# Windowed attention feeding a routed expert layer: where a running count is taken, an order of its own behind the last slot, and a normalization moved between engines

## Chip, core and metric

The kernel runs on one core of a Trainium2 chip. The metric is the device time of one execution, in microseconds (us), as the median of three executions. The engines are PE (TensorE, matrix products), DVE (VectorE), ACT (ScalarE), POOL (GpSimd) and SP (SyncE, which here only issues transfers). Each engine works through its own queue in order.

## The reference, cut to what matters

```
# attention: 8 batches, 8 heads, 576 positions, head size 64, window of 128 positions
scores = where(0 <= i - j < 128, q k^T / 8 - slope_h * |i - j|, -1e9)
x = softmax(scores) @ v                       # (8, 576, 512)
# expert layer: 8 experts, hidden size 1024
logits = x @ w_gate
for every token: fresh = argmax(logits)
    e = fresh if first of its batch or sigmoid(x . w_local) < 0.5 else e of the token before
    out = softmax(logits)[e] * (relu(x @ w1[e]) @ w2[e])
```

Each token goes to one expert, so the second half is a gather of token rows by expert, two matrix products, and a scatter.

## The kernel before, in words

**Attention.** Two heads make a pair and a batch has four pairs, so there are 32 pairs, numbered 0 to 31. The work of a pair is cut into atoms, each a letter and a block number: S (scores, PE), D (bias and row minimum, DVE), E (exponential and row sum, ACT), A and R (reciprocal of the sums: POOL, then DVE), N (the pieces of the block row times the reciprocal, nine in all, N3 four and N8 five), U (transposes, PE), C (their copy out of PSUM, DVE or ACT), M and H (products with v, PE), X (copy into the tile `xT`) and T (32x32 transposes of `xT` into the tile `T`, DVE). After a batch's fourth pair, T0 and T1 are each followed by a transfer of `T` to DRAM (`xd`): 1024 KB for T0, 128 KB for T1. There is one tile `T`, so a T of the next batch waits until these transfers have read it.

**Slots.** A slot emits one list of atoms, a software pipeline: an atom with k marks (`M3'''` has three) belongs to the pair k-1 before that of an unmarked one. `ORDER` holds the lists for the four pairs of a batch. Behind the last pair `LAST` holds what the pipeline still owes. Every engine gets its instructions in the order in which the atoms stand (`InOrder`, whose helper is L170 in the profile).

**Side work.** A `.` in a list takes one step of a generator, `side`: `tokens(b)` computes logits of a finished batch and `route(b)` the expert of each token, its rank among that expert's tokens (with `ohs`, the running count by expert) and the lists of rows. `;`, `:` and `,` take steps of `early()`, `gathers()` and `turns()`, which prepare the rows of the first expert before attention ends. `early()` rounds the count of an expert up to a whole tile at three points, after batches 3, 4 and 5: one PE product adds `ohs` up over partitions (`pn`), and three DVE operations follow. All these small PSUM results use one bank, `ptk` with `bufs=1`, so PE can write the next only when the last one has been read.

**Experts.** `Fixed.run` goes over eight pieces f of the hidden size: twelve products h (`three` four times), a relu on ACT (`hh`) and DVE (`hl`, L1101), and then nine products y of the piece before. Weights are loaded as `wraw` (512 KB), split by ACT (cast) and DVE (L246, the low part), two halves for each. `hl` lies where `T` lay, so the second `hl` waits until the last transfer out of `T` has landed. `Feed.tick` takes steps of `routing()` (tokens and route of the last batch, then the lists of all experts), gathers rows on POOL (L185) and turns them on DVE (L191, L195).

Of the kernel before, what the change touches and what calls it, by code (L numbers as in the profile page):

```python
# [8 lines left out]
F32 = mybir.dt.float32  # L9
# [4 lines left out]
ALU = mybir.AluOpType  # L14
AX = mybir.AxisListType
PS = bass.MemoryType.PSUM
P = 128

NB = 8
S = 576  # L20
DM = 512
NE = 8
NT = 5
KS = 4
NS = 3
# [11 lines left out]
EARLY = [[(2, 4), (3, 5)], [(3, 6)]]  # L37
# [13 lines left out]
def windows(nb):  # L51
    last = nb % 4
    if last in (1, 2):
# [14 lines left out]
]  # L68
DEPTH = 4
FIRST = "S0 S2 D2 D0 D1 D3 S8 D8 S4 S6 E8"  # L70
LAST = ["E2' M3''' E1' T1'''' D6' D4' C0''' . D5' D7' E0' . H2''' H0''' H3''' N8'' H1''' N3'' M1''' E3' E6' E5' E7' M0''' . U2'' E4' A3' C2'' U3'' . C3'' U1'' A8' T0'''' X0''' X1''' U0'' M2'' C1'' R3' R8'",
# [3 lines left out]
POOL_CUT = 19  # L75
PACE = 16
GROUP = 3
# [5 lines left out]
def moe_attention(ctx, tc, qT, kT_d, vv, wg, wl, w1, w2, out):  # L83
# [6 lines left out]
    tp = ctx.enter_context(tc.tile_pool(name="tok", bufs=2))  # L90

    sh = ctx.enter_context(tc.tile_pool(name="shared", bufs=2))
    ptk = ctx.enter_context(tc.tile_pool(name="ptk", bufs=1, space=PS))
# [11 lines left out]
    onesb = cp.tile([P, P], F16, name="onesb")  # L105
# [20 lines left out]
    ohs = st.tile([P, NE], F16, name="ohs")  # L126
    g32 = st.tile([P, 32], F32, name="g32")
    tbl = st.tile([P, 4 * NS * KS], F32, name="tbl")
# [17 lines left out]
    def chain(*gens):  # L146
        for g in gens:
            yield from g

    def run(g):  # L150
        for _ in g:
            pass
# [23 lines left out]
    pe, dve, act, pool = (InOrder(e) for e in (nc.tensor, nc.vector, nc.scalar, nc.gpsimd))  # L176
# [168 lines left out]
    with ExitStack() as actx:  # L345
# [168 lines left out]
        class Scores:  # L514


            def __init__(self, b, p, q, k):
                self.p, self.q, self.k, self.pbs = p, q, k, PB[(4 * b + p) % 2]
                self.mn = sp.tile([P, 9], F32, name="mn", bufs=3)
                self.sm = sp.tile([P, 9], F32, name="sm", bufs=3)  # L520
                self.r = sp.tile([P, 9], F32, name="r", bufs=3)
                self.ps, self.sc = {}, {}
# [43 lines left out]

            def N(self, i):
                for j in range(0, 4) if i == 3 else range(4, 9):
                    pool.tensor_scalar(self.part(j), self.part(j), self.r[:, j:j + 1], 1.0, ALU.mult, ALU.mult)

        class Weigh:
# [80 lines left out]
        def route(b):  # L652
            L = logits_of.pop(b)
            l8 = L[:, :, 0:NE]
            OH, RO = oh_all[:, b], ro_all[:, b]
# [36 lines left out]
            dve.tensor_tensor(OH, ph, k8, ALU.is_equal)  # L692
            yield

            assert all((e, k) in known for e, parts in enumerate(EARLY) for k, n in parts if n <= b)
            pr = ptk.tile([P, NT, NE], F32, name="pk")
            pe.matmul(pr, utri, OH, start=True, stop=False)
            for t in range(1, NT):
# [16 lines left out]
            for a in range(4):  # L715
                n = NT if a < 2 else NT - 1
# [24 lines left out]
                if t % 2:  # L741
                    yield
            yield
            pT = ptk.tile([P, 4 * NS * KS], F32, name="pk")
            for t in range(NT):
                pe.matmul(pT, RO[:, t], cw[:, t].rearrange("p e k -> p (e k)"), start=t == 0, stop=t == NT - 1)
            yield
            enter(tbl, pT, b)
            routed.append(b)
            yield  # L750

        def enter(table, ps, b):

            base = float(S * (b - b % GROUP))
            if base:
                z = tp.tile([P, P], F32, name="tz")[:, :table.shape[1]]
                dve.tensor_scalar(z, ps, 0.0, base, ALU.is_gt, ALU.mult)
            dve.tensor_tensor(table, table, ps, ALU.add)
            if base:
                dve.tensor_tensor(table, table, z, ALU.add)  # L760
# [43 lines left out]
        def early():  # L804

            parts = [(n, e, k, k0) for e, own in enumerate(EARLY) for (k, n), (k0, _) in zip(own, [(0, 0)] + own)]
            for n, e, k, k0 in sorted(parts):
                while n - 1 not in routed:
                    yield
                pn = ptk.tile([P, NE], F32, name="pk")  # L810
                pe.matmul(pn, onesb, ohs, start=True, stop=True)
                d = tp.tile([P, 1], F32, name="ed")
                dve.tensor_scalar(d, pn[:, e:e + 1], -1.0, float(k * P), ALU.mult, ALU.add)
                dve.tensor_scalar(d, d, 0.0, None, ALU.max)
                dve.tensor_tensor(ohs[0:1, e:e + 1], ohs[0:1, e:e + 1], d[0:1], ALU.add)
                yield
                at = 4 * KS * e + 4 * k0
                yield from indices(tbl[:, at:at + 4 * (k - k0)], idx0, at, KS * e + k0, windows(4 * (k - k0)))
                known.append((e, k))
# [53 lines left out]
        for slot in range(4 * NB + DEPTH):  # L873
# [30 lines left out]
                loaded = load(b + 1)  # L904
            if p == 2 and b + 1 < NB:
                load_v(b + 1)
        run(chain(prep[";"], prep[":"], prep[","], side))
        last_xT = xT


# [279 lines left out]
    class Flex:  # L1190
        n = 1
# [85 lines left out]
    route_done, rank_done, table_done, beyond = [], [], [], []  # L1277

    def routing():
        yield from chain(tokens(NB - 1, last_xT), route(NB - 1))  # L1280
        e = len(OWN) - 1
        yield from indices(tbl[:, 4 * KS * e:4 * KS * e + 4 * KS], idxs, 0, 0, windows(4 * KS))
        route_done.append(1)
        yield
        yield from rank_tables()
        table_done.append(1)
# [132 lines left out]
```

## Time and profile before

| | us |
|---|---|
| median of 3 | 667.01 (666.23 to 667.06) |
| the profiled execution: its own time | 666.91 |
| its span, first to last instruction | 665.1 |
| PE busy | 636.6 (96%), mean granted clock 0.982 |
| DVE busy | 455.5 (68%) |
| ACT busy | 393.4 (59%) |
| POOL busy | 390.5 (59%) |

The profiled execution stands 0.10 below the median, and 1.8 us of its time lie outside the span. The shares are averages over a kernel of two halves: attention ends at about 222 us, and what follows is expert work.

### The profile page before, as it was taken

To read this page: it belongs to the slowest core of one execution; us is meant where nothing else is said; L and a number is where in the kernel's file an instruction comes from. 1 tells how busy PE (TensorE), PEld (TensorE's weight loads), DVE (VectorE), ACT (ScalarE), POOL (GpSimd) and SP (SyncE) were. 2 spreads that over 40 slices of the span, in tenths; PEclk is the share of its full clock that TensorE was granted. 3 is DMA by queue.
4 is the path that set the end of the run, shared out by engine and by line. 5 is a ranking of instruction groups with operands and counts; after the bars stand their busy time and mean duration, and the time that the engine had idled before them with its cause. 6 is when DMAs were issued, how large, how long until landed. Compare 5 with 4: busy or idle time off the path is not lost. (4 is left out here: it accounts for less than half of the span.)

```text
span 665.1 us, 18079 instructions
## 1 busy us (share of the span) xinstructions
PE 636.6 (96%) x6414; PEld 526.2 (79%) x6414; DVE 455.5 (68%) x1623; ACT 393.4 (59%) x1177; POOL 390.5 (59%) x651
## 2 busy tenths in 40 slices
PE   8899999999977899999999999999999999999994
PEld 4677777776755688888887898888988899889883
DVE  4679999999996788994654374637464667854531
ACT  7899999988976444353443353535353565653430
POOL 6866666667859741776777575765253476615021
PEclk9999999999986999999999999999999999999998
DMA  8976765665212654557424673448333488448420
GB/s 274 369 260 204 234 188 182 210 194 184 81 51 78 204 175 150 189 178 238 133 69 150 206 247 96 138 155 269 124 114 117 145 264 318 143 136 298 158 85 30
DMA packets 59757, 117.01 MB, mean 176 GB/s; under 512 B 9132, under 2 KB 28076, under 8 KB 59664
## 3 DMA queue, kind: packets, MB, share of 16 engines
q1 hardware_dynamic: 50096, 95.93, 44.1%
q0 software_dynamic: 9136, 19.30, 8.9%
q8 instruction: 52, 0.85, 0.5%
q10 hardware_dynamic: 432, 0.59, 0.3%
q14 instruction: 41, 0.34, 0.2%
HBM read 96.84 MB, written 19.29 MB: 175 GB/s over the span
## 5 line engine op out<-in xcount | busy, mean ns | idle before, releaser
L185 POOL DMA_INDIRECT kr<-xd,xidx x136 | 147.4, 1084 | 52.1 <-issue 37.3
L1048 PE MATMUL h<-qx,cut 128*128 128x384 f32 (+6 forms) x408 | 136.2, 334 | 0.0
L170 POOL TENSOR_SCALAR cut<-cut,r 128x192 f32<-128x192 f32 (+2 forms) x288 | 114.4, 417 | 35.2 <-DVE r L170 15.3
L246 DVE TENSOR_TENSOR cut<-wraw,cut 128x512 fp32r<-128x512 f32 x171 | 110.8, 686 | 34.5 <-ACT cut L244 29.4
L1050 PE MATMUL h<-qx,cut 128*128 128x384 f32 (+6 forms) x408 | 134.4, 329 | 0.0
L1049 PE MATMUL h<-qx,cut 128*128 128x384 f32 (+6 forms) x408 | 134.2, 329 | 0.0
L170 ACT ACTIVATE cut<-scs,mn 128x192 f32<-128x192 f32 (+2 forms) x288 | 123.1, 433 | 6.0 <-DVE mn L170 4.5
L1042 POOL DMA_INDIRECT out<-y,sidx x41 | 45.4, 1108 | 133.9 <-ACT y L1057 65.3
L1100 ACT ACTIVATE hh<-h 128x384 fp32r<-128x384 f32 (+3 forms) x96 | 44.4, 463 | 126.3 <-PE h L1050 125.3
L1101 DVE SCALAR_TENSOR_TENSOR hl<-h,hh 128x384 fp32r<-128x384 f32 (+3 forms) x104 | 54.2, 521 | 93.1 <-ACT hh L1100 90.0
L1048 PE MATMUL y<-cut,hh 128*128 128x512 f32 x288 | 114.1, 396 | 0.0
L1049 PE MATMUL y<-cut,hh 128*128 128x512 f32 x288 | 114.1, 396 | 0.0
L1050 PE MATMUL y<-cut,hl 128*128 128x512 f32 x288 | 113.6, 395 | 0.0
L244 ACT CAST cut<-wraw 128x512 fp32r<-128x512 f32 x148 | 84.2, 618 | 26.9 <-PE y L1050 24.7
L170 DVE CUSTOM_DVE_ANT_0 scs<-sc,bias 128x192 f32<-128x192 f32 (+2 forms) x288 | 84.1, 318 | 6.8 <-PE sc L170 5.8
L1048 PEld LDWEIGHTS h<-qx,cut 128*128 128x128 f32 x408 | 77.0, 189 | 8.7 <-issue 4.1
L1049 PEld LDWEIGHTS h<-qx,cut 128*128 128x128 f32 x408 | 77.0, 189 | 4.3
L1050 PEld LDWEIGHTS h<-qx,cut 128*128 128x128 f32 x408 | 76.9, 189 | 1.9
L1050 PEld LDWEIGHTS y<-cut,hl 128*128 128x128 f32 x288 | 54.5, 189 | 11.9
L170 PE MATMUL pt<-ident,cut 128*128 128x128 f32 x384 | 60.7, 289 | 2.9 <-POOL cut L170 2.8
L170 PE MATMUL sc<-kr,qx 64*64 64x192 f32 (+2 forms) x1280 | 62.0, 303 | 1.0 <-DVE mn L170 0.6
L1048 PEld LDWEIGHTS y<-cut,hh 128*128 128x128 f32 x288 | 54.5, 189 | 9.1 <-issue 0.4
(214 smaller groups left out, 1079.8 us busy)
## 6 DMA issues: line engine op xcount, KB each, us to landing
wraw<-w SPq DMA_DIRECT2D x92, 512.0 KB
xT<-w SPq DMA_DIRECT2D x20, 512.0 KB
kr<-kT SPq DMA_DIRECT2D x31, 288.0 KB
qx<-qT SPq DMA_DIRECT2D x30, 288.0 KB
cut<-v SPq DMA_DIRECT2D x8, 1024.0 KB
xd<-T SPq DMA_DIRECT2D x8, 1024.0 KB
kr<-xd,xidx POOLq DMA_INDIRECT x136, 3.7
cut<-v SPq DMA_DIRECT2D x8, 128.0 KB
```

The source lines that it names most:

```text
L170: ins = getattr(self.engine, name)(*args, **kw)
L185: queued(nc.gpsimd.indirect_dma_start(out=r, out_offset=None, in_=src[0:n, :], in_offset=bass.IndirectOffsetOnAxis(ap=col, axis=0), bounds ...
L244: scalar.copy(c[:, 0, f], raw[:, f])
L246: (pool if 2 * n + f == POOL_CUT else vector).tensor_tensor(c[:, 1, f], raw[:, f], c[:, 0, f], ALU.subtract)
L1042: queued(nc.gpsimd.indirect_dma_start(out=out.rearrange("t (a c) -> (t a) c", a=n), out_offset=bass.IndirectOffsetOnAxis(ap=col, axis=0), ...
L1048: nc.tensor.matmul(o, ah, bh, start=start, stop=False)
L1049: nc.tensor.matmul(o, ah, bl, start=False, stop=False)
L1050: nc.tensor.matmul(o, al, bh, start=False, stop=stop)
L1100: now.act.activation(hh, hp[:, :M], AF.Relu)
L1101: nc.vector.scalar_tensor_tensor(hl, hp[:, :M], 0.0, hh, ALU.max, ALU.subtract)
```

## The change

Three things change. First, the product that counts (`pn`) leaves `early()` and is made at the end of `route(b)`, in further columns of the tile `pT` that takes the lists; the three DVE operations follow there. Second, `DEPTH` goes from 4 to 1: the four lists of `LAST` become one, in which pairs 28 to 31 stand mixed and a `.` comes after every six atoms; what is left of `side` behind it is no longer run out at once but handed to `routing()`. Third, the nine N pieces of pair 31 are DVE operations instead of POOL ones.

```diff
-DEPTH = 4
+DEPTH = 1
...
-        ". M3''' T1'''' C0''' . H2''' H0''' H3''' N8'' T0'''' H1''' N3'' M1''' . M0''' U2'' C2'' . U3'' C3'' U1'' X0''' X1''' U0'' M2'' C1'' .",
...
+LAST = ["T0'''' M1''' N3'' E0' M3''' E1' . H1''' H2''' T1'''' H3''' C0''' E2' . E3' D4' M0''' N8'' D5' H0''' . E4' U0'' D6' X1''' X0''' C0'' . E5' E6' T0''' M0'' A3' U1'' . T1''' D7' U2'' R3' C1'' N3' . U3'' C2'' M1'' C3'' U0' M2'' . E7' C0' M3'' H0'' A8' H1'' . H2'' R8' H3'' N8' X0'' X1'' . M0' U1' T0'' U2' C1' U3' . T1'' C2' M1' C3' M2' M3' . H0' H1' H2' H3' X0' X1' . T0' T1'"]
...
+                self.last = 4 * b + p >= 4 * NB - 1
...
             def N(self, i):
                 for j in range(0, 4) if i == 3 else range(4, 9):
+                    if self.last:
+                        dve.tensor_scalar(self.part(j), self.part(j), self.r[:, j:j + 1], None, ALU.mult)
+                        continue
                     pool.tensor_scalar(self.part(j), self.part(j), self.r[:, j:j + 1], 1.0, ALU.mult, ALU.mult)
...
-            pT = ptk.tile([P, 4 * NS * KS], F32, name="pk")
+            pT = ptk.tile([P, 4 * NS * KS + NE], F32, name="pk")
             for t in range(NT):
-                pe.matmul(pT, RO[:, t], cw[:, t].rearrange("p e k -> p (e k)"), start=t == 0, stop=t == NT - 1)
-            yield
-            enter(tbl, pT, b)
+                pe.matmul(pT[:, :4 * NS * KS], RO[:, t], cw[:, t].rearrange("p e k -> p (e k)"), start=t == 0, stop=t == NT - 1)
+            full = [(e, k) for e, parts in enumerate(EARLY) for k, n in parts if n == b + 1]
+            if full:
+                pe.matmul(pT[:, 4 * NS * KS:], onesb, ohs, start=True, stop=True, skip_group_check=True)
+            yield
+            enter(tbl, pT[:, :4 * NS * KS], b)
+            for e, k in full:
+                d = tp.tile([P, 1], F32, name="ed")
+                at = 4 * NS * KS + e
+                dve.tensor_scalar(d, pT[:, at:at + 1], -1.0, float(k * P), ALU.mult, ALU.add)
+                dve.tensor_scalar(d, d, 0.0, None, ALU.max)
+                dve.tensor_tensor(ohs[0:1, e:e + 1], ohs[0:1, e:e + 1], d[0:1], ALU.add)
             routed.append(b)
             yield
...
-                pn = ptk.tile([P, NE], F32, name="pk")
-                pe.matmul(pn, onesb, ohs, start=True, stop=True)
-                d = tp.tile([P, 1], F32, name="ed")
-                dve.tensor_scalar(d, pn[:, e:e + 1], -1.0, float(k * P), ALU.mult, ALU.add)
-                dve.tensor_scalar(d, d, 0.0, None, ALU.max)
-                dve.tensor_tensor(ohs[0:1, e:e + 1], ohs[0:1, e:e + 1], d[0:1], ALU.add)
-                yield
...
-        run(chain(prep[";"], prep[":"], prep[","], side))
+        run(chain(prep[";"], prep[":"], prep[","]))
+        rest = side
...
     def routing():
-        yield from chain(tokens(NB - 1, last_xT), route(NB - 1))
+        yield from chain(rest, tokens(NB - 1, last_xT), route(NB - 1))
```

How this moves instructions is shown at three places. The first is DVE's queue at the end of slot 31, the last slot with scores, from the routing step `rcb` of batch 6 on. Before:

```order
L170 TENSOR_TENSOR rcb<-rc,rf 128x5
L170 STREAM_TRANSPOSE T<-xT 128x2x32
L170 ISA scs,mn<-sc,bias 128x192
L170 ISA mn 128x1
L170 TENSOR_TENSOR xT<-wraw,xT 128x512
L170 ISA scs,mn<-sc,bias 128x192
L170 ISA mn 128x1
L170 COPY pts<-pt 128x384
```

With the change (lines of the helpers stand three lower there, L167 for L170):

```order
L167 TENSOR_TENSOR rcb<-rc,rf 128x5
L167 STREAM_TRANSPOSE T<-xT 128x16x32
L167 TENSOR_TENSOR xT<-wraw,xT 128x512
L167 STREAM_TRANSPOSE T<-xT 128x2x32
L167 COPY pts<-pt 128x384
L167 TENSOR_TENSOR xT<-wraw,xT 128x512
L167 SCALAR_TENSOR_TENSOR hr_99<-hold,pk 1x512
L167 ISA scs,mn<-sc,bias 128x192
```

The 16-block transpose into `T` (T0 of pair 28, the first pair of batch 7), which stood eleven instructions further on, is now the first behind `rcb`; the D atoms of pair 31 (`scs,mn`) stand behind it.

The second place is DVE's queue where pair 31 is normalized (`cut` times `r`). Before, these nine rows were POOL's. With the change:

```order
L167 RECIPROCAL r<-r 128x4
L167 TENSOR_SCALAR cut<-cut,r 128x64
L192 TENSOR_TENSOR qx<-xtr,qx 128x4x128
L167 TENSOR_SCALAR cut<-cut,r 128x128
L167 TENSOR_SCALAR cut<-cut,r 128x192 x2
L167 TENSOR_TENSOR rex<-L,rm 128x40
L167 TENSOR_TENSOR oh_all<-pk,k_85 128x40
L167 COPY pts<-pt 128x384
```

N3 stands as three rows there, and N8 follows in the same way behind the next reciprocal.

The third place is the first expert, where PE turns the logits of batch 7 (`pk<-ident,part`, five products, the fifth after DVE has read the first four, `L<-pk`). PE before:

```order
L1050 MATMUL h<-qx,cut 128x384
L1048 MATMUL h<-qx,cut 128x384
L1049 MATMUL h<-qx,cut 128x384
L1050 MATMUL h<-qx,cut 128x384
L1048 MATMUL h<-qx,cut 128x384
L170 MATMUL pk<-ident,part 128x128
L1049 MATMUL h<-qx,cut 128x384
L1050 MATMUL h<-qx,cut 128x384
```

PE with the change:

```order
L1051 MATMUL y<-cut,hh 128x512
L1052 MATMUL y<-cut,hh 128x512
L1053 MATMUL y<-cut,hl 128x512
L1051 MATMUL h<-qx,cut 128x384
L167 MATMUL pk<-ident,part 128x128
L1052 MATMUL h<-qx,cut 128x384
L1053 MATMUL h<-qx,cut 128x384
```

The fifth product stood behind seven of the twelve products h of piece f=2; it now stands behind those twelve, the nine products y of f=1 and one product h of f=3. DVE before, from the first `hl`:

```order
L1101 SCALAR_TENSOR_TENSOR hl<-h,hh 128x384
L246 TENSOR_TENSOR cut<-wraw,cut 128x512 x2
L1101 SCALAR_TENSOR_TENSOR hl<-h,hh 128x384
L246 TENSOR_TENSOR cut<-wraw,cut 128x512 x4
L170 TENSOR_REDUCE L<-pk 128x36
```

DVE with the change, from the last rows of batch 7 in `T`:

```order
L167 STREAM_TRANSPOSE T<-xT 128x16x32
L167 STREAM_TRANSPOSE T<-xT 128x2x32
L167 TENSOR_SCALAR ro_all<-rep_91,rrf,val 128x128 x3
L167 TENSOR_SCALAR tz<-pk 128x48
L167 TENSOR_TENSOR tbl<-tbl,pk 128x48
L167 TENSOR_TENSOR tbl<-tbl,tz 128x48
L1104 SCALAR_TENSOR_TENSOR hl<-h,hh 128x384
L243 TENSOR_TENSOR cut<-wraw,cut 128x512 x2
L1104 SCALAR_TENSOR_TENSOR hl<-h,hh 128x384
L243 TENSOR_TENSOR cut<-wraw,cut 128x512 x6
L1104 SCALAR_TENSOR_TENSOR hl<-h,hh 128x384
L243 TENSOR_TENSOR cut<-wraw,cut 128x512 x2
```

The row `L<-pk` stands next behind these. Between the second `hl` and it there were four splits (L246) and are now six, a third `hl` and two more splits.

## Rows read from the trace of the kernel before

**Rows 1.** Busy time by engine, ten-microsecond stretches (stretch, length, busy and count each, PE's granted clock).

```profile
core 0: us, PE busy (x) PEld busy (x) DVE busy (x) ACT busy (x) POOL busy (x), PEclk, DMA share, GB/s
...
200.00:210.00 10.00, 6.45 (x86) 4.41 (x83) 6.20 (x17) 7.44 (x26) 8.97 (x15) 0.73 0.39 116
...
240.00:250.00 10.00, 10.00 (x60) 8.69 (x59) 8.23 (x28) 4.15 (x9) 1.30 (x1) 1.00 0.32 100
```

**Rows 2.** Who waited for whom on PE: total us, times, longest.

```profile
PE pk L170 <- DVE tbl L170: 3.4, 3, 2.4
PE pk L170 <- DVE L L170: 2.9, 1, 2.9
```

**Rows 3.** PE in order of time: start, us, and idle time before (in brackets).

```profile
27.12 0.27 PE L170 MATMUL xa<-pts,cut 64*64 64x64 f32 x2 [1.76 <-DVE pts L170]
...
190.68 0.17 PE L170 MATMUL pk<-ohs,onesb 128*128 128x8 f16 x1 [2.37 <-DVE tbl L170]
...
230.74 0.33 PE L170 MATMUL pk<-ident,part 128*128 128x128 f32 x1 [2.93 <-DVE L L170]
```

**Rows 4.** PE busy and its granted clock behind the first two of these.

```profile
core 0: us, PE busy (x), PEclk, DMA share, GB/s
...
28.00:30.00 2.00, 2.00 (x35) 1.00 1.03 403
...
192.00:194.00 2.00, 2.00 (x14) 0.50 0.03 10
```

**Rows 5.** DVE in order of time, end of slot 31.

```profile
195.32 0.36 DVE L170 CUSTOM_DVE_ANT_0 scs<-sc,bias 128x192 f32<-128x192 f32 x1 [0.56 <-PE sc L170]
...
195.88 0.70 DVE L170 STREAM_TRANSPOSE T<-xT 128x512 f32<-128x512 f32 x1
...
199.33 0.17 DVE L170 TENSOR_TENSOR rcb<-rc,rf 128x5 f16<-128x5 f32 x1
```

**Rows 6.** SP's issues of the 1024 KB transfers out of T, batches 6 and 7.

```profile
196.61 0.38 SPq L627 DMA_DIRECT2D xd<-T  x1
...
221.98 0.39 SPq L627 DMA_DIRECT2D xd<-T  x1
```

**Rows 7.** DVE in order of time, end of attention and start of the first expert.

```profile
218.89 1.25 DVE L170 TENSOR_SCALAR ro_all<-rep,rrf,val 128x128 f16<-128x128 f16 x5
...
220.69 0.16 DVE L170 TENSOR_SCALAR tz<-pk 128x48 f32<-128x48 f32 x1
...
221.12 0.83 DVE L170 STREAM_TRANSPOSE T<-xT 128x64 f32<-128x64 f32 x2
221.88 0.52 DVE L1101 SCALAR_TENSOR_TENSOR hl<-h,hh 128x384 fp32r<-128x384 f32 x1
...
227.50 0.56 DVE L1101 SCALAR_TENSOR_TENSOR hl<-h,hh 128x384 fp32r<-128x384 f32 x1 [2.55 <-DMA xd<-T]
227.98 2.49 DVE L246 TENSOR_TENSOR cut<-wraw,cut 128x512 fp32r<-128x512 f32 x4
230.38 0.30 DVE L170 TENSOR_REDUCE L<-pk 128x36 f32<-128x144 f32 x1
```

**Rows 8.** DVE's busy time from the end of slot 31 to the first hl.

```profile
core 0: us, DVE busy (x), PEclk, DMA share, GB/s
199.41:221.88 22.47, 16.99 (x61) 0.77 0.29 86
```

**Rows 9.** Groups of instructions: a DVE scaling of an SBUF tile, and POOL's N pieces.

```profile
L170 DVE TENSOR_SCALAR bias<-rel 64x256 f32<-64x256 f32 x2 | 0.6, 302 | 2.6 <-POOL rel L170 2.5
L170 POOL TENSOR_SCALAR cut<-cut,r 128x192 f32<-128x192 f32 x224 | 93.8, 435 | 35.2 <-DVE r L170 15.3 <-PE pt L170 10.3 <-DVE ti L170 9.3
```

**Rows 10.** PE in order of time, first and tenth product after the wait for L: nine products y.

```profile
231.79 0.57 PE L1048 MATMUL y<-cut,hh 128*128 128x512 f32 x1
...
235.43 0.34 PE L1048 MATMUL h<-qx,cut 128*128 128x384 f32 x1
235.61 0.34 PE L1049 MATMUL h<-qx,cut 128*128 128x384 f32 x1
```

**Rows 11.** The third expert: its list (DVE), scatter and last of 16 gathers (POOL), first product (PE).

```profile
257.57 0.23 DVE L170 TENSOR_SCALAR xidx<-fi,roff 128x16 int32<-128x16 f32 x1
...
263.46 1.03 POOL L1042 DMA_INDIRECT out<-y,sidx  x1 [4.38 <-ACT y L170]
...
287.61 1.95 POOL L185 DMA_INDIRECT kr<-xd,xidx  x1 [0.30 <-issue]
...
298.69 0.39 PE L1048 MATMUL h<-qx,cut 128*128 128x512 f32 x1
```

More of the change, by code (lines that the diff above doesn't have):

```diff
@@ L68 @@
 ]
-DEPTH = 4
+DEPTH = 1
 FIRST = "S0 S2 D2 D0 D1 D3 S8 D8 S4 S6 E8"
-LAST = ["E2' M3''' E1' T1'''' D6' D4' C0''' . D5' D7' E0' . H2''' H0''' H3''' N8'' H1''' N3'' M1''' E3' E6' E5' E7' M0''' . U2'' E4' A3' C2'' U3'' . C3'' U1'' A8' T0'''' X0''' X1''' U0'' M2'' C1'' R3' R8'",
[3 rows of a table removed]
+LAST = ["T0'''' M1''' N3'' E0' M3''' E1' . H1''' H2''' T1'''' H3''' C0''' E2' . E3' D4' M0''' N8'' D5' H0''' . E4' U0'' D6' X1''' X0''' C0'' . E5' E6' T0''' M0'' A3' U1'' . T1''' D7' U2'' R3' C1'' N3' . U3'' C2'' M1'' C3'' U0' M2'' . E7' C0' M3'' H0'' A8' H1'' . H2'' R8' H3'' N8' X0'' X1'' . M0' U1' T0'' U2' C1' U3' . T1'' C2' M1' C3' M2' M3' . H0' H1' H2' H3' X0' X1' . T0' T1'"]
 POOL_CUT = 19
@@ L693, in route @@
             yield
-            assert all((e, k) in known for e, parts in enumerate(EARLY) for k, n in parts if n <= b)
             pr = ptk.tile([P, NT, NE], F32, name="pk")
```

2 rows, old and new, of the table LAST are left out of this document.

## The prediction

> **What bounds the kernel now.** I read the busy time by stretches first. From 240 us on PE works without a break (10.00 of 10.00 us, granted clock 1.00, which is 2.4 GHz), and so it stays nearly to the end; between 200 and 210 us, where attention drains, PE is busy 6.45 of 10 us at a mean clock of 0.73 [rows 1]. So the end of the kernel moves by whatever PE gains or loses before about 240 us, as long as the later expert work is never starved. PE's waits show two of interest: 3.4 us in three waits on the table `tbl`, which are the three counts of `early()`, and 2.9 us in one wait for `L` [rows 2]. In order of time, the longest count wait ends at 190.68, after 2.37 us, and the wait for `L` at 230.74, after 2.93 us [rows 3]. A wait costs more than itself when the clock falls behind it: after the 2.37 us the clock is 0.50 (1.2 GHz) at 192 to 194 us, while after a wait of 1.76 us that ended at 27.12 it stayed 1.00 [rows 3, 4]. The same fall stands behind the wait for `L`: nine products y take 231.79 to 235.43, 3.64 us [rows 10], where nine at the full clock take 2.1 (an estimate from the last rows there: products of 384 columns start 0.18 us apart, so of 512 columns 0.24).
>
> **The count.** It removes no work: the product and three small DVE operations per count stay. What goes is PE standing before the bank until DVE has put the lists into `tbl`. PE does not get 3.4 us for that. DVE is what PE waits for there, and the next product into that bank, the logits of batch 6, still has to wait until DVE has read lists and count. What DVE itself can win in slot 31 is its wait for PE of 0.56 us at 195.32 [rows 5]. I take that, less about 0.3 us for list operations that now come ahead of the T transpose of 195.88: that transpose ends some 0.2 us earlier, and the transfer that SP issued at 196.61 [rows 6] goes at about 196.4. If the three waits were returned in full it would be 3.4 us; both ends stay for the range.
>
> **The head of DVE's queue.** With the change the 16-block transpose of pair 28 follows `rcb`, which ends at 199.5 [rows 5]. It overwrites `T`, so it must wait until the 1024 KB of batch 6 have left. How long that transfer takes is read from its twin: issued at 221.98, it let the second `hl` start at 227.50, so 5.5 us [rows 6, 7]. Issued at 196.4 it frees `T` at 201.9. DVE then stands still for about 2.5 us, and behind it in the queue stand both splits of the expert's weights, the copy `pts` that PE's M0 needs, the scan of the routing, and the D atoms of pair 31. Before, a small transpose stood there that did not wait.
>
> **DVE's work from there.** Between 199.41 and the first `hl` at 221.88 DVE is busy 16.99 of 22.47 us, so it idles 5.5 us [rows 8]. The same operations stand behind the transpose now, plus the nine N pieces. No row shows N on DVE. The nearest DVE row scales 256 elements from SBUF to SBUF in 302 ns; the nine pieces hold 1536 elements, which is 1.8 us by elements and 2.7 by instructions (9 x 0.302). I take 2.1. POOL's own price is the upper bound, 9 x 0.435 = 3.9 [rows 9]; the lower is half of the element count, 0.9. For waits between engines that a queue this full still has (the copy of U0 of pair 31 waits for PE) I add an estimate of 0.5. First `hl`: 201.9 + 17.0 + 2.1 + 0.5 = 221.5, against 221.88. So the tail itself comes out nearly even: what mixing the pairs saves, DVE gives back in the wait at its head and in the nine pieces.
>
> A rule of the Trainium skill speaks about the price. "VectorE: DVE Perf Modes" (Mode 2×_2P — use both read ports for one tensor) says that a scaling of one fp32 tensor in SBUF writes two results a cycle; the row above, 302 ns for 256 elements, is nearer to one. By the rule the nine pieces would be about 1 us cheaper (an estimate) and the sum lower by as much; I keep the row.
>
> **The first expert.** The last 16-block transpose into `T` now stands ahead of the small one, three of the five `ro_all` and the table update. These took 0.2, 0.75 (three fifths of 1.25) and 0.4 us [rows 7], so it ends at 221.5 - 1.4 = 220.1, is issued at 220.15 as the first of the two transfers, and lands 5.5 us later at 225.65 (before: 227.50). Then DVE runs to `L`: `hl` 0.5, six splits 3.6 (four took 2.40, from 227.98 to 230.38), the third `hl` 0.5, two splits 1.2, `L` 0.3 [rows 7]. That is 6.1 us, and `L` is there at 231.75, a microsecond later than before (230.68). But PE has done more by then: the last five products h of f=2, the nine y of f=1 and the first h of f=3. Before, PE was at that point, about to start the second h of f=3, at 235.61 [rows 10]. With the change it is there at 231.75 + 0.05 + 0.1 (the fifth product into the bank) = 231.9, if the clock holds behind the wait. Gain 3.7 us.
>
> Does it hold? PE's work from the first `hl` to that point is 18 products y and 13 h (18 x 0.235 + 13 x 0.175 = 6.5 us), with logits and transposes 0.8 more, after `hl` at 222.0: PE arrives at 229.3 and waits 2.4 us. That is nearest to the 2.37 us after which the clock fell, not to the 1.76 us after which it held [rows 3, 4]. I take the fall, 3.64 - 2.1 = 1.5 us as before. Gain 3.7 - 1.5 = 2.2 us.
>
> **What hides the rest.** The rest of the routing of batch 6 is no longer run out at once, so routing of batch 7 and the lists come about one piece f later in PE's order, some 4.3 us. The cover: the third expert's list was there at 257.57, the gathers were held back by the scatter at 263.46, and 16 of them were issued by 289.6, while PE needs the rows at 298.69 [rows 11]. With the change the scatters come first and the gathers follow in one run, so 262 is early enough. Beyond some 8 us of delay the third expert would start late.
>
> **Sum.** The profiled execution took 666.91 us, 0.10 below the median. 666.9 - 2.2 = **664.7 us**.
>
> **Rivals.**
> 1. *The clock holds* behind the wait for `L`, because it comes out nearer 1.8 than 2.4 us (a microsecond off either way is within the sums above): 666.9 - 3.7 = 663.2.
> 2. *The count comes back.* PE, not DVE, sets slots 22, 26 and 30, and the 3.4 us of [rows 2] return in full, no low clock at 192 us included: 664.7 - 3.4 = 661.3. Against it: DVE was the one waited for.
> 3. *No change.* DVE takes POOL's price for N (1.8 us more), which moves the first `hl`, the last transfer and `L` alike: 664.7 + 1.8 = 666.5, within 0.2% of before. For it: DVE is the full queue of this stretch and takes work from an engine with a later deadline.
> 4. *Slower.* DVE's pieces and POOL's gathers shut each other out. In the changed order POOL starts its gathers (about 1.0 us each, 1.3 apart) just when DVE does N8. If each of the five pieces waits for one gather, DVE is 5 us later, `L` too: 664.7 + 5 = 669.7. It decides against the change once the nine pieces together cost over about 4.3 us (2.1 and the gain of 2.2). Against it: the five scalings `ro_all` at 218.89 took 0.25 us each, with no sign of being held [rows 7]. "SBUF — State Buffer" of the Trainium skill (SBUF: two separate sides) has this rule: the two engines share a pair of ports as an exclusive lock, for a DVE operation in a two-port mode among others. Whether N runs in one no row shows.
>
> **Chances.** Forecast 0.37, rival 1 0.20, rival 2 0.14, rival 3 0.17, rival 4 (and late lists) 0.12. What a measurement of this kernel can tell from no change is about 0.2%, 1.3 us. The forecast's own range is 663.4 to 666.2: a landing of 5.0 to 5.9 us counts twice (0.5 each way), N 0.9 to 2.7 us. Faster by over 0.2% (below 665.6): rivals 1 and 2 and most of the forecast, 0.69. Within: rival 3 and the rest of the forecast, 0.20. Slower: 0.11. The range of 8 in 10 leaves out rival 4 and the far end of rival 2: 661.4 to 667.2.
>
> **What would show it.** Right: no wait on `tbl` among PE's waits; an idle DVE of about 2.5 us ahead of the 16-block transpose at 199.5, put down to the transfer out of `T`; pieces `cut<-cut,r` of 0.2 to 0.3 us on DVE; the first `hl` near 221.5, the second near 225.7; a wait for `L` of about 2 us on PE and a clock of 0.50 behind it. Wrong: DVE not idle at 199.5 (then the gain is larger by up to 2.5 us), pieces of 0.5 us or more, PE waiting before 298 us for the third expert, or a new wait of PE for weights, because SP issues the third chunk behind other transfers.

## The result, and the profile after

The changed kernel took 673.59 us in the median of four runs (671.51 to 676.66), the kernel before 666.78 in four of its own. The ratio is 1.010, interval 1.0074 to 1.0126: slower by 1%, 6.8 us, where 664.7 us had been forecast. The profiled execution took 674.19 us, its span is 672.4. Lines of the helpers are numbered 3 lower than before, those of the expert part 3 higher.

First the busy time by stretches of the changed kernel (columns as in [rows 1]).

```profile
core 0: us, PE busy (x) PEld busy (x) DVE busy (x) ACT busy (x) POOL busy (x), PEclk, DMA share, GB/s
200.00:210.00 10.00, 6.03 (x50) 4.28 (x50) 8.59 (x25) 4.40 (x16) 5.00 (x8) 0.59 0.25 75
...
290.00:300.00 10.00, 8.02 (x31) 6.24 (x30) 6.98 (x32) 3.86 (x7) 6.88 (x7) 0.87 0.39 120
300.00:310.00 10.00, 6.42 (x20) 4.41 (x19) 5.94 (x22) 2.94 (x5) 4.55 (x6) 0.79 0.85 311
```

The kernel before, in the same stretches:

```profile
290.00:300.00 10.00, 10.00 (x49) 8.67 (x48) 9.83 (x41) 6.08 (x12) 7.87 (x8) 1.00 0.69 227
300.00:310.00 10.00, 10.00 (x45) 8.28 (x45) 5.29 (x13) 3.02 (x7) 6.10 (x6) 1.00 0.90 308
```

The new hole is at 290 to 310 us, where the kernel before was busy throughout: PE is idle for 5.6 of 20 us, and its clock is down to 0.79. PE's waits name what is missing there (total us, times, longest):

```profile
PE h L1051 <- ACT qx L191: 3.6, 1, 3.6
...
PE pk L167 <- DVE L L167: 1.0, 1, 1.0
```

The waits for `tbl` are gone, the wait for `L` is 1.0 instead of 2.9 us [rows 2], and PE now waits for `qx`, the turned rows of the third expert. Around that wait, the changed kernel in order of time, picked from the queues of DVE, POOL, ACT and PE:

```profile
259.77 0.23 DVE L167 TENSOR_SCALAR xidx<-fi,roff 128x16 int32<-128x16 f32 x1
...
261.57 1.03 POOL L1045 DMA_INDIRECT out<-y,sidx  x1 [15.63 <-ACT y L167]
267.17 0.99 POOL L1045 DMA_INDIRECT out<-y,sidx  x1 [4.57 <-DVE z L1013]
268.47 1.04 POOL L182 DMA_INDIRECT kr<-xd,xidx  x1 [0.31 <-issue]
...
291.32 1.00 POOL L182 DMA_INDIRECT kr<-xd,xidx  x1 [0.31 <-issue]
...
293.44 0.71 DVE L188 STREAM_TRANSPOSE xtr<-kr 128x512 f32<-128x512 f32 x1 [3.02 <-DMA kr<-xd,xidx]
...
300.70 1.14 ACT L241 CAST cut<-wraw 128x512 fp32r<-128x512 f32 x2 [1.87 <-PE y L1053]
...
302.83 0.70 DVE L188 STREAM_TRANSPOSE xtr<-kr 128x512 f32<-128x512 f32 x1
...
303.56 0.62 ACT L191 CAST qx<-xtr 128x512 fp32r<-128x512 f32 x1 [1.14 <-DVE xtr L188]
...
304.24 1.22 PE L1051 MATMUL h<-qx,cut 128*128 128x512 f32 x2 [3.58 <-ACT qx L191]
```

The list (`xidx`) was there at 259.77, only 2.2 us later than before [rows 11]. But the first gather starts at 268.47, since two scatters stand ahead of it in POOL's queue, and the second stood 4.57 us behind the first. DVE then waits 3.02 us for the third tile's rows. The turn of the fourth tile (DVE's transpose `xtr` and ACT's copy `qx`) stands, in both queues, behind a split of weights that itself waits for PE's last product `y` of the second expert, so PE cannot start before that split, the transpose and the copy are done.

The tail of attention, DVE in order of time, and SP's issue of batch 6 out of `T`:

```profile
195.04 0.38 SPq L628 DMA_DIRECT2D xd<-T  x1
...
200.28 0.71 DVE L167 STREAM_TRANSPOSE T<-xT 128x512 f32<-128x512 f32 x1 [2.92 <-ACT cut L167]
...
221.32 0.84 DVE L167 STREAM_TRANSPOSE T<-xT 128x512 f32<-128x512 f32 x2 [2.23 <-ACT xT L167]
...
223.94 0.21 DVE L167 TENSOR_SCALAR tz<-pk 128x48 f32<-128x48 f32 x1 [1.14 <-PE pk L167]
...
224.42 0.55 DVE L1104 SCALAR_TENSOR_TENSOR hl<-h,hh 128x384 fp32r<-128x384 f32 x1
```

And the busy time from that transpose to the first `hl`:

```profile
core 0: us, PE busy (x) PEld busy (x) DVE busy (x) ACT busy (x) POOL busy (x), PEclk, DMA share, GB/s
200.28:224.42 24.14, 20.29 (x201) 15.28 (x201) 19.04 (x68) 10.80 (x30) 14.66 (x18) 0.65 0.27 81
```

The wait of 2.92 us at the head is there, and DVE is then busy for 19.04 us. The row puts the wait down to ACT, but it ended as the 1024 KB that were issued at 195.04 landed: the last number of the following line is the median from issue to landing of these transfers, and 195.04 + 5.2 is 200.24.

```profile
xd<-T SPq DMA_DIRECT2D x8, 1024.0 KB, 5.2
```

PE works at half its clock in this stretch, but so it did in the kernel before, for less long. First two stretches of before, then the same two with the change:

```profile
205.00:215.00 10.00, 7.84 (x88) 6.21 (x89) 6.29 (x19) 4.14 (x11) 8.86 (x18) 0.51 0.21 67
215.00:225.00 10.00, 10.00 (x119) 7.39 (x116) 7.79 (x30) 5.36 (x14) 7.87 (x8) 1.00 0.47 138
```

```profile
205.00:215.00 10.00, 8.94 (x95) 6.39 (x93) 8.42 (x30) 6.20 (x18) 2.94 (x5) 0.50 0.14 47
215.00:225.00 10.00, 10.00 (x102) 7.64 (x98) 6.48 (x29) 4.10 (x10) 7.79 (x7) 0.81 0.46 137
```

In finer steps the clock stands at 0.50 from 206 to 214 us before, and from 202 to 218 us with the change.

To compare executions, these are the starts in us of marks in the traces; the runs are told below.

| | before | changed | e1 | e2 | e3 | e4 | e15 |
|---|---|---|---|---|---|---|---|
| batch 0's first transfer out of `T` | 41.45 | 40.16 | 43.09 | 41.45 | 41.51 | 42.66 | 41.42 |
| batch 6's 1024 KB out of `T` | 196.61 | 195.04 | 197.81 | 196.53 | 196.70 | 197.18 | 196.58 |
| first `hl` | 221.88 | 224.42 | 227.43 | 226.22 | 225.15 | 222.03 | 221.12 |
| last h of the second expert | 294.40 | 292.17 | 296.48 | 293.97 | 293.54 | 294.03 | 292.33 |
| first h of the third expert | 298.69 | 304.24 | 300.78 | 302.00 | 297.83 | 304.59 | 296.63 |
| span | 665.1 | 672.4 | 667.2 | 670.6 | 664.3 | 673.8 | 663.1 |

Read it downwards. The changed kernel's lead of 1.3 us stands already at 41 us, before anything that the change touches: it is chance, and executions differ there by up to 2.9 us. Against before it gains 0.3 us more up to batch 6's transfer, loses 4.1 us from there to the first `hl`, wins 4.8 up to the end of the second expert, loses 7.8 at the third expert, and 1.8 more behind it at the low clock.

### The profile page after: what moved, and what is told of

Same layout as the page of the kernel before. It is cut to its first block, busy times and chain, and to the rows that moved or that the text cites. A ratio compares the mean times of both kernels' runs of the same rounds, so it can differ in the third digit from the quotient of the medians.

```text
span 672.4 us, 18074 instructions
## 1 busy us (share of the span) xinstructions
PE 638.7 (95%) x6414; PEld 527.0 (78%) x6414; DVE 457.4 (68%) x1632; ACT 393.5 (59%) x1177; POOL 385.8 (57%) x642
## 5 line engine op out<-in xcount | busy, mean ns | idle before, releaser
L182 POOL DMA_INDIRECT kr<-xd,xidx x136 | 149.7, 1101 | 42.4 <-issue 37.9
L167 POOL TENSOR_SCALAR cut<-cut,r 128x192 f32<-128x192 f32 (+2 forms) x279 | 108.1, 409 | 35.7 <-DVE r L167 14.6
L167 ACT ACTIVATE cut<-scs,mn 128x192 f32<-128x192 f32 (+2 forms) x288 | 123.2, 433 | 8.3 <-DVE mn L167 8.3
L167 DVE CUSTOM_DVE_ANT_0 scs<-sc,bias 128x192 f32<-128x192 f32 (+2 forms) x288 | 83.8, 317 | 4.7 <-PE sc L167 4.3
L167 PE MATMUL pt<-ident,cut 128*128 128x128 f32 x384 | 61.5, 292 | 2.9 <-POOL cut L167 2.1
L167 PE MATMUL sc<-kr,qx 64*64 64x192 f32 (+2 forms) x1280 | 61.2, 301 | 2.9 <-DVE mn L167 2.4
```

What stands on the lines that cost most here:

```text
L167: ins = getattr(self.engine, name)(*args, **kw)
L182: queued(nc.gpsimd.indirect_dma_start(out=r, out_offset=None, in_=src[0:n, :], in_offset=bass.IndirectOffsetOnAxis(ap=col, axis=0), bounds ...
```

## The experiments

The first four ran on one chip, where the kernel before took 666.95 us (23 runs).

**e1: the list at its old place.**

```diff
         def tick(self, upto, turn=True):
             self.clock += 1
             next(self.side, None)
+            if self.clock <= 4:
+                next(self.side, None)
```

> The changed kernel, in which the side work of batch 6 and the routing of batch 7 take two steps at each of the first four ticks of the experts, so that the third expert's list stands again where it stood before the change. Theory A (all that the change loses lies in the third expert's rows, because its list comes four ticks later): PE stood 2.2 us ahead of the kernel before at 292 us of the changed kernel (the nine products y of f=6 begin at 292.35 there, at 294.57 before) and keeps that, so 666.9 - 2.2 = 664.7 us, between 663.2 and 666.2. PE has no wait for qx, and the first gather of the third expert stands ahead of the first scatter. Rival T (the tail is to blame: the idle 2.9 us of DVE at 200 us and the clock of 0.56 behind it come back as a loss later on): 669 us or more, whatever the list does. Rival S (the steps taken at once cost PE what the list gains, since the first expert then waits for the routing chain): 666 to 668 us.

667.32 us, ratio 1.0004 (0.9992 to 1.0016). The loss of 1% is gone, and so is the wait for `qx`. In its trace the first gather again stands ahead of the scatters:

```profile
260.07 1.01 POOL L182 DMA_INDIRECT kr<-xd,xidx  x1 [10.26 <-DVE xidx L167]
265.45 1.02 POOL L1045 DMA_INDIRECT out<-y,sidx  x1 [4.38 <-ACT y L167]
```

But it isn't the 664.7 us of theory A: with the list in its place the change is worth nothing. The forecast's gain is missing too, and that is a second question (e5 to e18). The time lies in the range of rival S as well; the trace gives S little room, since from the first `hl` to the third expert e1 takes 73.35 us and e3, in which no step is doubled, 72.68.

**e2: scatters held; e3: and the turn earlier.** The list stays late in both. e2 changes the first line, e3 both:

```diff
-            if pending and self.clock % 3 == 0:
+            if pending and self.clock % 3 == 0 and not 33 <= self.clock < 51:
...
-                if x[0] <= upto and self.clock >= x[2] + lag:
+                if x[0] <= upto and self.clock >= x[2] + (min(lag, 6) if x[0] == 2 else lag):
```

> The changed kernel with the list where the change puts it, but no scatter is issued between ticks 33 and 50, so that the third expert's gathers are not behind the first expert's scatters in GpSimd's queue. Theory A1 (the loss is the gathers, which stood behind two scatters of which the second waits 4.6 us for the first to land, so that DVE waits 3.0 us for the rows of the third tile): the first gather moves from 268.5 to about 260.3, DVE no longer waits, and PE loses nothing: 664.7 us. Theory A2 (the loss is the place of the fourth tile's turn, which the late list puts behind the split of weights that waits for PE's last product y of the second expert): PE still waits 3.6 us for qx, behind an end of the second expert that is not late any more: the third expert starts at 296.5 + 3.6 = 300.1 (before: 298.69), plus some 1.7 us of half clock behind so long a wait: 666.9 + 1.4 + 1.7 = 670.0 us. Both half and half would lie between. Rival T (the tail): no change from the changed kernel, 673.6 us.

> As the run with the scatters held, and the turns of the third expert's tiles come 6 ticks behind their last gather in place of 10, so that the fourth tile's turn stands ahead of the split that waits for PE's last product y. The list stays where the change puts it. Theories A1 and A2 together (gathers behind scatters, and the last turn behind that split, are all of the loss): no wait of PE for qx, 664.7 us, 663.2 to 666.2. If A1 alone is right, the same as the run with the scatters held; if A2 alone, some 3 to 5 us less than that run. Rival T (the tail): 669 us or more.

e2: 672.2 us, ratio 1.0080 (1.0060 to 1.0101). The gathers start right behind the list (`xidx` 261.65, first gather 262.16), DVE's four transposes of rows no longer wait for them, and PE still waits as long as in the changed kernel. ACT and PE of e2:

```profile
298.46 1.14 ACT L241 CAST cut<-wraw 128x512 fp32r<-128x512 f32 x2 [0.67 <-PE y L1053]
...
301.33 0.62 ACT L191 CAST qx<-xtr 128x512 fp32r<-128x512 f32 x1 [1.15 <-DVE xtr L188]
...
302.00 0.73 PE L1051 MATMUL h<-qx,cut 128*128 128x512 f32 x2 [3.58 <-ACT qx L191]
```

e3: 666.37 us, ratio 0.9996 (0.9983 to 1.0009). Here the copy stands ahead of that split, and PE goes on without a wait. ACT and PE of e3:

```profile
294.87 0.62 ACT L191 CAST qx<-xtr 128x512 fp32r<-128x512 f32 x1
...
297.83 0.39 PE L1051 MATMUL h<-qx,cut 128*128 128x512 f32 x1
...
298.03 1.14 ACT L241 CAST cut<-wraw 128x512 fp32r<-128x512 f32 x2 [0.67 <-PE y L1053]
```

So A2 is right: the place of the fourth tile's turn behind that split is 5.8 us (672.2 less 666.4). What A1 is worth is less sure. By the times the late gathers make up 0.2% between the changed kernel and e2, which the intervals don't separate. By the marks above, the stretch from the last h of the second expert to the first h of the third is 12.07 us in the changed kernel and 8.03 in e2, so in these two executions the late gathers cost 4.0 us there. The early turn without held scatters was not run, so what the late gathers cost with the turn in its place stays open.

**e4: the late list in the kernel before.**

```diff
+        for _ in range(4):
+            yield
         e = len(OWN) - 1
         yield from indices(tbl[:, 4 * KS * e:4 * KS * e + 4 * KS], idxs, 0, 0, windows(4 * KS))
```

> The kernel before with one edit: four ticks of nothing ahead of the indices of the third expert's list, so that its list comes as late as in the changed kernel, and nothing of attention or of the count is touched. Theory A (the late list is enough for all of the loss): the third expert starts late by what the changed kernel lost from 292 us on, 2.2 + 7.0 = 9.2 us, since the scatters that hold its gathers wait for PE's own products and move along with it: 666.9 + 9.2 = 676 us, at least 671. Rival T (the tail loses it): the four ticks are covered, 667 us.

675.61 us, ratio 1.0136 (1.0114 to 1.0157): 8.7 us lost where 9.2 were expected, with attention and counts untouched. POOL and PE of e4:

```profile
263.47 1.03 POOL L1042 DMA_INDIRECT out<-y,sidx  x1 [15.65 <-ACT y L170]
268.91 0.99 POOL L1042 DMA_INDIRECT out<-y,sidx  x1 [4.41 <-DVE sq L967]
270.21 1.04 POOL L185 DMA_INDIRECT kr<-xd,xidx  x1 [0.30 <-issue]
...
304.59 1.23 PE L1048 MATMUL h<-qx,cut 128*128 128x512 f32 x2 [4.15 <-ACT qx L194]
```

The same queue and the same wait: four ticks of lateness are enough for a loss of this size. This is shown from both sides, e1 and e4.

**The parts of the tail, in runs with other times (e5 to e14, e16 to e18).** Each undoes one thing in e3, and the diffs of two stand here: the transposes moved, and N on GpSimd. The third puts the count back into a bank of its own; the last is the count's edit alone in the kernel before.

```diff
-LAST = ["T0'''' M1''' N3'' ... H2''' T1'''' H3''' C0''' ... E6' T0''' M0'' A3' ...
+LAST = ["M1''' N3'' ... H2''' H3''' C0''' ... E6' T0'''' T1'''' T0''' M0'' A3' ...
```

```diff
-                self.last = 4 * b + p >= 4 * NB - 1
+                self.last = False
```

> The run with the scatters held and the early turn (666.4 us), in which the two transposes of pair 28 into T no longer stand at the head of the order behind slot 31, where DVE waits 2.9 us for the transfer out of T, but ahead of those of pair 29. Theory H (that wait, and the 3.3 us that PE then waits for pts with the clock of 0.50 behind it, are what eats the gain in the tail): DVE's idle 2.9 us at 202 us goes, PE's wait for pts falls below 1 us, the first hl comes 2 to 4 us earlier, and the time is 662.4 to 664.4 us. Rival D (PE sets the tail from there, and DVE only waits elsewhere, for xT and pk): 665.8 to 667.0 us, PE's clock as low as before.

> The run with the scatters held and the early turn (666.4 us), with the nine pieces N of the last pair on GpSimd again. Theory P (the prediction's term: DVE is the full queue of the tail and its 2.1 us of N lie on the path): DVE is 2.1 us earlier at the first hl, 664.3 us. Rival Q (DVE waits behind N for xT and pk anyway, 2 us and more, so that N on DVE costs nothing): 666.4 us, within 0.6. Rival R (GpSimd is slower and its gathers stand in its queue, so that the copies of U wait for N): 667.5 us or more.

> The run with the scatters held and the early turn (666.4 us), with the three counts in a bank of their own again, after the lists, as before the change. Theory of the prediction (DVE is what PE waits for there; the edit gives only DVE's 0.6 us, with 0.2 back for the list work): 667 us, at most 667.4. Rival 2 of the prediction (the whole 3.4 us of the waits come back with the edit): 669 to 670 us. PE shows three waits for tbl again in either case.

> The kernel before, with the count's edit alone: the product of the count goes into the bank of the lists. Theory of the prediction: 0.4 to 0.9 us faster than before (667.0), 666.1 to 666.6. Rival 2 (the 3.4 us of PE's three waits for tbl come back, with the half clock behind the longest): 663.6 us. A loss of over 0.5 us would say that the edit hurts, since early() now writes ohs later in DVE's queue, behind the lists.

In these runs and their repeats the kernel before itself took 744 to 759 us in the median, 11 to 14% more than its usual time:

| runs, kernel before | transposes moved | N on GpSimd | count in its own bank | count alone |
|---|---|---|---|---|
| e5 to e8, 759.24 us | 1.0185 (1.0116 to 1.0255) | 1.0187 (1.0125 to 1.0249) | 1.0244 (1.0186 to 1.0302) | 0.9979 (0.9932 to 1.0027) |
| e9 to e12, 746.35 us | 1.0115 (1.0045 to 1.0186) | 1.0081 (1.0030 to 1.0132) | 1.0195 (1.0149 to 1.0241) | 0.9859 (0.9793 to 0.9924) |
| e13, e14, 743.55 us | 1.0169 (1.0043 to 1.0295) | | | 742.6 us, no ratio |
| e16 to e18, 754.55 us | 1.0217 (1.0161 to 1.0273) | 1.0214 (1.0158 to 1.0269) | 1.0285 (1.0223 to 1.0347) | |

> Once more the run with the scatters held, the early turn, and the two transposes of pair 28 into T ahead of those of pair 29, on a chip with the usual times (the first went to one on which the kernel before took 759 us). The base without the moved transposes took 666.4 us. Theory H (DVE's idle 2.9 us at the head of its queue, and the clock of 0.50 behind PE's wait for pts, eat the gain in the tail): 662.4 to 664.4 us. Rival D (PE sets the tail, DVE only waits elsewhere): 665.8 to 667.0 us.

> Once more the run with the scatters held, the early turn, and the nine pieces N of the last pair on GpSimd again, on a chip with the usual times. The base took 666.4 us. Theory P (DVE's 2.1 us of N lie on the path): 664.3 us. Rival Q (DVE waits behind N anyway): 666.4 us, within 0.6. Rival R (GpSimd is slower, and its gathers stand ahead of N in its queue): 667.5 us or more.

> Once more the run with the scatters held, the early turn, and the three counts in a bank of their own again, on a chip with the usual times. The base took 666.4 us. Theory of the prediction: 667 us, at most 667.4. Rival 2 of the prediction (all of the 3.4 us come back with the edit): 669 to 670 us.

> Once more the kernel before with the count's edit alone, on a chip with the usual times. Theory of the prediction: 0.4 to 0.9 us faster than before (667.0). Rival 2: 3.4 us faster, or more by the half clock behind the longest wait. On the slow chip it was faster by 0.2% with an interval of 0.5% to either side, which tells neither apart.

> The run with the scatters held and the early turn (666.4 us where the kernel before took 667.0), with the two transposes of pair 28 into T moved to stand ahead of those of pair 29; the two runs of it so far fell on a chip with other times. Theory H (DVE's idle 2.9 us at the head of its queue, PE's 3.3 us behind it and the clock of 0.50 behind that eat the gain in the tail): 662.4 to 664.4 us, and the first hl 2 to 4 us earlier. Rival D (PE sets the tail, DVE only waits elsewhere): 665.8 to 667.0 us.

> The kernel before with the count's edit alone, on a chip with the usual times. Theory of the prediction: 0.4 to 0.9 us faster than before (667.0). Rival 2 of the prediction: 3.4 us faster, or more by the half clock behind the longest wait. Within 0.3 us of before: the edit gives nothing, since DVE, for which PE waits there, is no earlier.

> The run with the scatters held and the early turn (666.4 us where the kernel before took 667.0), with the two transposes of pair 28 into T moved to stand ahead of those of pair 29. Theory H (DVE's idle 2.9 us at the head of its queue, PE's 3.3 us behind it and the clock of 0.50 behind that eat the gain in the tail): 662.4 to 664.4 us, and the first hl 2 to 4 us earlier. Rival D (PE sets the tail, DVE only waits elsewhere): 665.8 to 667.0 us.

> The run with the scatters held and the early turn (666.4 us), with the nine pieces N of the last pair on GpSimd again. Theory P (DVE's 2.1 us of N lie on the path): 664.3 us. Rival Q (DVE waits behind N for xT and pk anyway, 2 us and more): 666.4 us, within 0.6. Rival R (GpSimd is slower, and its gathers stand ahead of N in its queue, so that the copies of U wait for N): 667.5 us or more.

> The run with the scatters held and the early turn (666.4 us), with the three counts in a bank of their own again. Theory of the prediction (the edit gives DVE's 0.6 us, less 0.2 for list work): 667 us, at most 667.4. Rival 2 of the prediction (the 3.4 us come back with the edit): 669 to 670 us. PE shows three waits for tbl again in either case.

None of these ratios answers for the usual times, and e3, in which the first three each undo one thing, was not run beside them. They show no more than that under such times every kernel with the new order was slower than the kernel before, by 0.8 to 2.9%, and the count alone was not. The engines stand there for long stretches with nothing to wait for in the profile; the largest such entry among the waits of all engines, first of e16, then of e3:

```profile
DVE hl L1104 <- issue: 71.7, 21, 22.9
```

```profile
POOL kr L182 <- issue: 37.2, 122, 0.3
```

Up to about 207 us, though, e16 runs like e3, and there it can be read. PE behind slot 31, first e3, then e16:

```profile
204.10 0.34 PE L167 MATMUL xb<-pts,cut 128*64 128x64 f32 x4 [3.27 <-DVE pts L167]
205.86 0.21 PE L167 MATMUL pk<-identb,rcb 128*1 128x64 f16 x1 [0.94 <-DVE hr L167]
207.55 0.49 PE L167 MATMUL xb<-pts,cut 128*64 128x64 f32 x4 [0.65 <-DVE pts L167]
209.66 0.29 PE L167 MATMUL pk<-onesb,hr 1*128 1x8 f16 x5
```

```profile
201.23 0.34 PE L167 MATMUL xb<-pts,cut 128*64 128x64 f32 x4 [0.56 <-DVE pts L167]
202.44 0.19 PE L167 MATMUL pk<-identb,rcb 128*1 128x64 f16 x1 [0.48 <-DVE hr L167]
204.72 0.34 PE L167 MATMUL xb<-pts,cut 128*64 128x64 f32 x4 [1.62 <-DVE pts L167]
206.88 0.27 PE L167 MATMUL pk<-onesb,hr 1*128 1x8 f16 x5 [0.65 <-DVE hr L167]
```

With the two transposes moved, PE has the five products of `hr` 2.8 us earlier: the wait at the head of DVE's queue does reach PE. In e5, e9 and e13, which are the same kernel, the first of these waits is 0.56 to 0.59 us too. The granted clock falls all the same (0.56 at 205 to 210 us in e16, 0.50 in e3), so the wait of 3.3 us isn't what it takes, and that part of theory H fails. Whether the 2.8 us last to the first `hl` isn't known.

**e15: the count alone, at the usual times** (the kernel before 667.08 us there).

> The kernel before with the count's edit alone, on a chip with the usual times (667.0 us for the kernel before). Theory of the prediction: 0.4 to 0.9 us faster than before. Rival 2 of the prediction: 3.4 us faster, or more by the half clock behind the longest wait. Within 0.3 us of before: the edit gives nothing, since DVE, for which PE waits there, is no earlier.

665.27 us in the median, ratio 0.9994 (0.9970 to 1.0017): inconclusive, since both kernels ranged over 5 to 6 us on this chip; a gain of 0.4 to 0.9 us lies within it, 3.4 us does not. The ratio isn't that of the two medians, which lie 1.8 us apart. The range goes with PE's mean granted clock. With the count alone, eight executions at 0.990 to 0.992 took 664.2 to 666.0 us and four at 0.977 to 0.982 took 667.4 to 670.6; of the kernel before, seven at 0.987 to 0.990 took 664.9 to 666.6 and ten at 0.980 to 0.985 took 667.1 to 669.8. Whether the edit makes the higher clock more frequent, these numbers are too few to show. PE of e15 at the wait for `L`, and the clock behind it:

```profile
229.96 0.33 PE L170 MATMUL pk<-ident,part 128*128 128x128 f32 x1 [2.72 <-DVE L L170]
```

```profile
core 0: us, PE busy (x) PEld busy (x) DVE busy (x) ACT busy (x) POOL busy (x), PEclk, DMA share, GB/s
230.00:234.00 4.00, 4.00 (x20) 3.41 (x20) 3.85 (x12) 2.23 (x5) 3.08 (x4) 1.00 0.86 257
```

Its span is 2.0 us shorter than that of the kernel before: 0.8 of it stands at the first `hl`, and 1.3 come behind the wait for `L`, where the clock held this time.

## Why the prediction was wrong

**The cover** is the step that failed: "With the change the scatters come first and the gathers follow in one run, so 262 is early enough. Beyond some 8 us of delay the third expert would start late." The delay was four ticks, one piece f, as forecast, and the list itself only 2.2 us later. Two things were not counted behind it. The second scatter stands 4.4 to 4.6 us at the head of POOL's queue (changed kernel, e4). DVE's small operation named as its releaser differs between the two. The starts of the first two scatters lie 5.4 to 6.0 us apart in six of the seven traces above, and 6.8 in e3, and the changed kernel's trace puts five other waits of scatters down to the landing of an earlier scatter (3.5 us together); so I take it to wait for the first to land, which no run tried by itself. And, worth more, a turn comes a set number of ticks behind its gathers, so the late list moved the last turn behind a split that waits for PE's last product of the second expert. The prediction asked when the data would be there and not what the late instructions would stand behind. The fourth turn alone was worth 5.8 us (e2 against e3), the gathers 1.4 by the times and 4.0 by the marks. Rival 4 had "late lists" in its bracket, without place or price.

**First `hl` at 221.5** was the second miss. It was 25.1 us behind the issue of batch 6's transfer by forecast (196.4); it took 29.4 us in the changed kernel, 29.6, 29.7 and 28.5 in e1, e2 and e3, and 24.5 with the count alone. The wait at the head came as forecast (2.92 us for about 2.5, the transfer 5.2 for 5.5), and so did DVE's work: busy 19.04 us, where the sum was 17.0 + 2.1. What was mis-sized is the 0.5 us for waits. DVE stood 5.1 us, nearly the 5.5 that it stood before [rows 8]; the forecast let mixing the pairs remove almost all of that, and it only moved the waits to other places. The longest is 2.23 for ACT's copies into `xT`, which in turn stood 1.76 us for PE's `xb`. PE's half clock, about twice as long as before, had no term in the sum, since it treated DVE as the only bound. That PE's wait of 3.3 us brought the clock down isn't shown: the clock fell in the kernel before as well, behind no single wait over 1.44 us, and in e16 behind 0.56, 0.48 and 1.62. Nor is it shown how much of the 5.1 us comes from the clock.

**N** took 0.25, 0.74 for three, 0.42 and 1.01 for four pieces, 2.4 us for 2.1. By size (the number ahead of the last bar is the mean ns of one):

```profile
L167 DVE TENSOR_SCALAR cut<-cut,r 128x192 f32<-128x192 f32 x7 | 2.0, 327 | 0.0
...
L167 DVE TENSOR_SCALAR cut<-cut,r 128x128 f32<-128x128 f32 x1 | 0.3, 279 | 0.0
L167 DVE TENSOR_SCALAR cut<-cut,r 128x64 f32<-128x64 f32 x1 | 0.3, 254 | 0.0
```

Without the one of 0.42, a piece of 192 elements took 0.31 us, only 0.06 more than one of 64: 0.4 to 0.5 ns for each further element, and some 0.2 us for each piece whatever its size. The row kept has 1.2 ns an element [rows 9]; the prediction called that nearer to one result a cycle, as if all of its 302 ns went by elements. By "VectorE: DVE Perf Modes" of the Trainium skill (Mode 2×_2P — use both read ports for one tensor), which gives two results a cycle, N was to be about a microsecond less. The trace speaks for that faster rate and not for the saving, since most of a piece's time doesn't depend on its size. Of rival 4's exclusion little shows: four pieces at 213.87 took 0.31 us each, one started every 0.23 us, while GpSimd issued a gather from 213.59 to 214.81; the one that took 0.42, at 212.93, ran beside one too.

**The first expert** gave back more than forecast. `L` was there 9.5 us behind the first `hl` (forecast 10.3), PE's wait for it was 0.96 us instead of 2.4, and the clock held, as rival 1 has it. The prediction chose between its two cases by the length of the wait, which the runs don't bear out: the clock fell behind 2.37 us [rows 3, 4], 2.93 and, in e4, 2.79, and it held behind 2.72 in e15. From the first `hl` to the end of the second expert the changed kernel was 4.8 us faster than before, where the forecast had 1.8. So the later `hl` and the shorter wait nearly cancel: e1 and e3 stand at the time of before, not 2.2 us below.

**The count** behaved as forecast in what it doesn't give: the waits for `tbl` went, and up to batch 6's transfer PE and DVE were no earlier by more than the 0.6 us by which executions differ there; rival 2's 3.4 us lie outside the interval of the count alone, which ends at 2.0 us faster (e15). Its own size stays open, as do the shares of the head wait, the order and N in the 4 us of the tail. At the usual times no kernel here is shown to beat the one before.

## What to carry over

When a change makes a list, a load or a table later in program order, ask which instructions move along with it, and behind which waits each of them then stands in its queue; the time at which the data are there is only half of the cover. If a schedule counts ticks from one step to the next, four ticks at its start are four ticks at its end, where there may be none. And a sum over one full queue has to say why the waits that this queue has now should go: DVE stood 5.5 us before the change and 5.1 with it, where 0.5 had been put down. A time divided by its elements is no rate either, until a row of another size shows what part of it goes by elements.

## What the runs showed of the hardware

The same instructions arrived at 41 us of the program up to 2.9 us apart in seven executions (40.16 to 43.09), so a lead of a microsecond between two traces has to be taken from a mark behind which they differ. After waits of 2.93 (before) and 2.79 us (e4) for `L` the clock fell, after one of 2.72 (e15) it held, and in the kernel before it fell after one of 2.37 us at 190.68; so the length of a wait alone doesn't tell. And in several runs the kernel before took 744 to 759 us instead of 667, while engines of the kernels beside it stood up to 22.9 us at a time (e16) for nothing but "issue"; what held their instructions back, these profiles don't say. It isn't shown to belong to a chip either: e16 to e18 bear the same chip number as e1 to e4.
